# Reads at the head of a two-layer kernel: two queues for the first, Pool for the rest, copies in halves

## The chip, the cores and the metric

The kernel runs on one core of a Trainium2 chip. The metric is device time in microseconds of one execution; the median of several executions counts.

## What is computed

The reference applies two layers, each of them attention and a gated unit with residuals, to 2048 tokens of 448 features in fp32 (16 heads of 28, hidden width 1792). Both layers use the same weights.

```python
def _A_ref(x, wqkv, wo):
    qkv = (x @ wqkv).reshape(B, S, 3, H, Dh).transpose(2, 0, 3, 1, 4)
    q, k, v = qkv[0], qkv[1], qkv[2]
    scores = jnp.einsum("bhqd,bhkd->bhqk", q, k) * (Dh ** -0.5)
    p = _softmax(scores, axis=-1)
    o = jnp.einsum("bhqk,bhkd->bhqd", p, v)
    return o.transpose(0, 2, 1, 3).reshape(B, S, D) @ wo
def _B_ref(x, w_gate, w_up, w_down):
    h = _sigmoid(x @ w_gate) * (x @ w_up)
    return h @ w_down
x = x + _A_ref(_layernorm(x), A_wqkv, A_wo)
x = x + _B_ref(_layernorm(x), B_w_gate, B_w_up, B_w_down)
# the same two lines once more
```

## The kernel before

The 2048 tokens stand as 16 tiles of 128 tokens; four tiles make a block, and there are four blocks. The product of a block with the weights is done in fp16: each operand is split into a high and a low half, and three products are added up. To fit fp16 the weights are scaled by a power of two that is worked out from the sum of their squares. Per layer there are four stages: query, key and value products of all blocks, attention, output product, gated unit. The order of the instructions is written out by hand; each engine (TensorE, VectorE, ScalarE, Pool, and SyncE for transfers) runs its own instructions strictly in that order, and semaphores tie the engines together.

The change is in the head, the work ahead of the first query product:

- `load_x` (line 176) reads tiles of tokens; `load_rows` (lines 211, 213, 214) reads 448 rows of a weight matrix as three slabs of 128 rows and a last one of 64 rows that is read twice. SyncE issues all of them: tokens of tiles 0 to 3 one by one, the query weights (the slabs in two transfers), the key weights, the tokens of block 1, the value weights, the tokens of blocks 2 and 3. Each transfer has one of eight semaphores, in turn, and the ninth waits for the first to have landed.
- `stats` (lines 495, 496) takes mean and variance of a tile on VectorE, and Pool makes the factor of it (498, 500). `scale` (320, VectorE) normalizes the tile, and `turn` (508) transposes it on TensorE, four transposes into four banks of PSUM. Each bank holds one slab of features of all four tiles. The order on VectorE is statistics 0 and 1, scale 0, statistics 2 and 3, scales 1, 2 and 3.
- `turned_high` (530 on VectorE, 532 on ScalarE) copies a bank to fp16, `turned_low` (540, 543) makes the low half.
- `measure_first` (620 on ScalarE, 617 on VectorE) takes the sums of squares of the query weights in three parts, `sum_first` (626) adds them over the partitions on TensorE, and two small operations on VectorE (246, 248) make the power of two.
- `scaled_high` (231, ScalarE) and `scaled_low` (234, VectorE) scale and split the weights by columns. The first query product (564) takes the first 128 columns. `measure` (633) later does for key and value weights in one operation each what `measure_first` does for the query weights.
- `keep_busy` (261) issues products of a zero tile to TensorE between the transposes.
- `tables` (190 to 204) and `ones_of_values` (719, 720) prepare constants on Pool.

## Time and profile before

| | us |
|---|---|
| median of 3 runs | 1894.93 |
| lowest and highest | 1894.68, 1895.23 |
| span of the profiled execution | 1893.0 |
| TensorE busy in it | 1886.5 (100%) |
| VectorE, ScalarE, Pool busy | 1430.7, 1382.7, 231.5 |

The span reaches from the first to the last instruction of one profiled execution; the execution's own time is not given apart from the runs, and its median lies 1.9 us above the span. A row of a timeline gives the start and the duration in us, the engine (PE is TensorE, PEld its loading of weights, DVE VectorE, ACT ScalarE, POOL Pool, SPq SyncE issuing a transfer), the line of the kernel, the operation, what it writes and reads, and in brackets how long the engine had stood idle before it and whose work released it. A row of waits gives the total, the count and the longest.

### The profile page before, as it was taken

Reading aid. Unit: us, or ns where it says so; the run is one execution under the profiler, and the core shown is the slowest. Engines: PE = TensorE matmul, PEld = TensorE weight load, DVE = VectorE, ACT = ScalarE, POOL = GpSimd, SP = SyncE. Lnnn points to the kernel's source line nnn. Section 1 sums busy time; section 2 is a strip of 40 time slices with the busy share of each in tenths; the row PEclk is TensorE's granted clock in tenths of the full one; section 3 lists DMA queues with packets and bytes.
Section 4 is the critical chain, followed back from the end, with each engine's and each line's share of the span. In section 5 each row is a group of like instructions: output and inputs, shape, how many; then the busy total and the mean of one; then the engine's idle time right before and its main releaser. Section 6 shows DMA issues by size and latency. Waiting matters only on the chain. (4 is left out here: it accounts for less than half of the span.)

```text
span 1893.0 us, 56282 instructions
## 1 busy us (share of the span) xinstructions
PE 1886.5 (100%) x24254; PEld 1323.1 (70%) x24254; DVE 1430.7 (76%) x2835; ACT 1382.7 (73%) x1772; POOL 231.5 (12%) x453
## 2 busy tenths in 40 slices
PE   9999999999999999999999999999999999999999
PEld 4455555555556799999954556667666567999998
DVE  7758989898976688787564487787778676887664
ACT  5569999999993566555345799999999745565541
POOL 3023112222101111111100000000000020121110
PEclk9999999999999999999999999999999999999999
DMA  7676454334323566646734322122120245666553
GB/s 247 194 212 166 132 137 128 107 119 129 103 88 121 192 205 235 231 181 238 251 96 134 90 52 47 32 52 52 31 48 24 67 160 174 218 251 223 208 208 142
DMA packets 110882, 270.86 MB, mean 143 GB/s; under 512 B 13214, under 2 KB 67838, under 8 KB 110496
## 3 DMA queue, kind: packets, MB, share of 16 engines
q0 software_dynamic: 31776, 158.51, 23.4%
q1 hardware_dynamic: 78288, 108.20, 20.3%
q8 instruction: 192, 3.15, 0.7%
q10 hardware_dynamic: 560, 0.46, 0.1%
q14 instruction: 66, 0.54, 0.1%
HBM read 207.88 MB, written 50.85 MB: 137 GB/s over the span
## 5 line engine op out<-in xcount | busy, mean ns | idle before, releaser
L1222 ACT ACTIVATE prob_s<-sc 128x1536 f32<-128x1536 f32 (+1 forms) x657 | 887.9, 1487 | 6.6 <-PE sc L1207 5.9
L1258 PE MATMUL acc<-prob_s,val_s 128*32 128x256 f32 (+3 forms) x7700 | 569.9, 383 | 0.0
L1207 PE MATMUL sc<-qp_s 114*32 114x512 f16 x7868 | 553.2, 379 | 0.0
L579 PEld LDWEIGHTS <-gu_s 128*128 128x128 f16 x4368 | 426.9, 98 | 46.8 <-issue 0.4
L1207 PEld LDWEIGHTS <-qp_s 114*32 114x32 f16 x8192 | 272.7, 95 | 203.4 <-issue 88.3
L1258 PEld LDWEIGHTS acc<-prob_s,val_s 128*32 128x32 f32 x7700 | 272.3, 110 | 142.9 <-issue 13.6
L579 PE MATMUL chain<-xwide_s,gu_s 128*128 128x256 f16 x2016 | 247.5, 273 | 0.0
L1552 PE MATMUL dnp<-dn_s,hparts_s 128*128 128x224 f16 x2016 | 225.2, 259 | 0.0
L1552 PEld LDWEIGHTS <-hparts_s 128*128 128x128 f16 x2016 | 194.0, 98 | 4.4
L1238 DVE SCALAR_TENSOR_TENSOR power_q<-power_q,expo_q 128x512 f32<-128x512 f32 x243 | 168.2, 692 | 8.3
L1625 ACT COPY one_q<-chain 128x256 f32<-128x256 f32 x224 | 82.4, 371 | 121.4 <-PE chain L579 120.8
L1641 DVE TENSOR_TENSOR one_q<-side,one_q 128x512 f32<-128x512 f32 x112 | 72.2, 686 | 101.8 <-PE side L579 101.5
L579 PE MATMUL side<-xshort_s,gu_s 128*128 128x256 f16 x1120 | 140.5, 273 | 0.0
L564 PE MATMUL qkp<-xhl_s,wqk_s 128*128 128x512 f16 x616 | 138.1, 379 | 0.7 <-ACT wqk_s L231 0.2
L564 PEld LDWEIGHTS <-wqk_s 128*128 128x128 f16 x616 | 60.1, 98 | 69.8 <-ACT wqk_s L231 1.1
L1437 POOL DMA_DIRECT2D gu_s<-gu_parts x104 | 56.0, 538 | 430.5 <-PE side L579 424.5
L1287 DVE STREAM_TRANSPOSE oturned_q<-acc 128x512 f32<-128x512 f32 x32 | 22.9, 716 | 97.1 <-PE acc L1258 96.9
L1258 PE MATMUL acc<-power_q,val_s 128*32 128x256 f32 (+3 forms) x300 | 94.2, 396 | 0.0
L579 PE MATMUL side<-xwide_s,gu_s 128*128 128x256 f16 x672 | 91.6, 273 | 0.0
L1505 ACT CAST hparts_s<-hsums_q 128x256 f16<-128x256 f32 (+1 forms) x136 | 65.0, 494 | 30.2 <-DVE hsums_q L1517 20.2
L756 ACT ACTIVATE qkhl_q<-qkp 128x512 f16<-128x512 f32 x56 | 33.2, 593 | 71.9 <-PE qkp L564 68.3
L1652 ACT ACTIVATE one_q<-one_q 128x512 f32<-128x512 f32 x56 | 35.2, 629 | 64.3 <-DVE one_q L1641 64.3
(218 smaller groups left out, 2318.0 us busy)
## 6 DMA issues: line engine op xcount, KB each, us to landing
gu_s<-gu_parts POOLq DMA_DIRECT2D x104, 800.0 KB, 6.0
dn_s<-dn_parts POOLq DMA_DIRECT2D x42, 784.0 KB, 7.8
qp_s<-qk_scr SPq DMA_DIRECT2D x96, 224.0 KB
qk_scr<-qkhl_q SPq DMA_DIRECT2D x56, 256.0 KB
gu_parts<-pack_s POOLq DMA_DIRECT2D x14, 800.0 KB, 3.8
xt_scr<-xs_s SPq DMA_DIRECT2D x48, 224.0 KB
xraw_s<-xt_scr SPq DMA_DIRECT2D x12, 768.0 KB
qp_s<-qk_scr SPq DMA_DIRECT2D x64, 112.0 KB
```

The lines of the kernel that those rows point to most:

```text
L564: nc.tensor.matmul(pm, w, x, start=(i == 0), stop=(i == len(terms) - 1))
L579: nc.tensor.matmul(pm, a, x, start=(first and i == 0), stop=(i == len(terms) - 1), skip_group_check=True)
L1207: nc.tensor.matmul(ps[32 * j:32 * j + 32, :], hd.k[:, keys], hd.q[:, qb * W:(qb + 1) * W], start=True, stop=True, tile_position=(0, 32 * j))
L1222: nc.scalar.activation(prob[:, 0:n, :], ps[:, 0:n, :], AF.Exp, scale=exp_scale)
L1238: nc.vector.scalar_tensor_tensor(p, p, c[k], y, op0=ALU.add, op1=ALU.mult)
L1258: nc.tensor.matmul(acc[qb * VC:(qb + 1) * VC, s], v[:, kc % TB, h, :], probs[c * NB + qb][:, s], start=(kc == 0 and a == 0), stop=(kc == N ...
L1437: queue.dma_start(self.gu[-1][m], gu_parts[p, m])
L1505: nc.scalar.copy(to[:, :, 0], a)
L1552: nc.tensor.matmul(pm, a[:, x, t], w[:, p, y], start=(begin and n == 0 and (j == 0 or alone)), stop=(n == 2), skip_group_check=True)
L1625: nc.scalar.copy(to, pm)
L1641: nc.vector.tensor_tensor(one[m], side[m], one[m], op=ALU.add)
L1652: nc.scalar.activation(out, v, AF.Sigmoid, scale=gate_scale)
```

## The change

SyncE issues the tokens of tiles 0 and 2 and the first two slabs of the query weights; ScalarE issues tiles 1 and 3 and the other parts of the query weights, ahead of its table load. All later reads are issued by Pool, in the order key weights, tokens of block 1, value weights, tokens of blocks 2 and 3, behind the factors of the four tiles and ahead of `tables`. The banks are copied to fp16 in two halves of two tiles each: ScalarE copies its three banks for tiles 0 and 1 behind the transposes of tile 1, VectorE copies the first bank for tiles 0 and 1 between scale 2 and scale 3. The first two sums of squares are taken on ScalarE behind these half copies, the second of them behind the half copies for tiles 2 and 3, and the three sums over the partitions stand together. Five products of `keep_busy` go away.

```diff
--- before.py
+++ after.py
@@ -172,12 +172,13 @@
     x_src = x_in[0].rearrange("(p t) d -> p t d", t=NT)
     x_dst = out[0].rearrange("(p t) d -> p t d", t=NT)
 
-    def load_x(t, n):
-        nc.sync.dma_start(x[:, t:t + n, :], x_src[:, t:t + n, :])
-
+    def load_x(t, n, queue=nc.sync):
+        queue.dma_start(x[:, t:t + n, :], x_src[:, t:t + n, :])
+
+    for t in range(TB):
+        load_x(t, 1, (nc.sync, nc.scalar)[t % 2])
     nc.vector.memset(still, 0.0)
     nc.vector.memset(warm, 0.0)
-    nc.scalar.activation(warm, warm, AF.Square)
     make_identity(nc, ident)
     nc.gpsimd.memset(nhalf, -0.5)
     nc.gpsimd.memset(ones, 1.0)
@@ -205,13 +206,13 @@
         big.put(units)
 
 
-    def load_rows(dst, src, c0, n, queue=nc.sync, parted=False):
-
-        for a, b in ((0, 2), (2, 3)) if parted else ((0, 3),):
-            queue.dma_start(dst[:, a:b, :],
-                            src[a * P:b * P, c0:c0 + n].rearrange("(s p) n -> p s n", p=P))
-        queue.dma_start(dst[0:64, 3, :], src[384:448, c0:c0 + n])
-        queue.dma_start(dst[64:128, 3, :], src[384:448, c0:c0 + n])
+    def load_rows(dst, src, c0, n, queue=nc.sync, second=None):
+
+        for a, b in ((0, 2), (2, 3)) if second else ((0, 3),):
+            (second if a else queue).dma_start(
+                dst[:, a:b, :], src[a * P:b * P, c0:c0 + n].rearrange("(s p) n -> p s n", p=P))
+        for r in (0, 64):
+            (second or queue).dma_start(dst[r:r + 64, 3, :], src[384:448, c0:c0 + n])
 
     def split(hi, lo, raw):
 
@@ -520,27 +521,29 @@
                 nc.scalar.copy(self.raw[0:n, kt, :], pt[0:n])
             big.put(self.xn)
 
-        def turned_high(self, kts=range(4), engine=None):
+        def turned_high(self, kts=range(4), engine=None, js=range(TB)):
+            c = slice(js[0] * P, (js[-1] + 1) * P)
             for kt in kts:
                 if kt not in self.pt:
                     continue
-                to, pt = ((self.hi[:, kt, :], self.pt[kt]) if kt < 3 else
-                          (self.tail[0:64], self.pt[kt][0:64]))
+                to, pt = ((self.hi[:, kt, c], self.pt[kt][:, c]) if kt < 3 else
+                          (self.tail[0:64, c], self.pt[kt][0:64, c]))
                 if engine is nc.vector:
                     nc.vector.tensor_copy(to, pt)
                 else:
                     nc.scalar.copy(to, pt)
 
-        def turned_low(self, kts=range(4)):
+        def turned_low(self, kts=range(4), js=range(TB)):
+            c = slice(js[0] * P, (js[-1] + 1) * P)
             for kt in kts:
                 if kt not in self.pt:
                     continue
-                pt = self.pt[kt]
+                pt = self.pt[kt][:, c]
                 if kt < 3:
-                    nc.vector.tensor_tensor(self.lo[:, kt, :], pt, self.hi[:, kt, :],
+                    nc.vector.tensor_tensor(self.lo[:, kt, c], pt, self.hi[:, kt, c],
                                             op=ALU.subtract)
                 else:
-                    nc.vector.tensor_tensor(self.tail[64:128], pt[0:64], self.tail[0:64],
+                    nc.vector.tensor_tensor(self.tail[64:128, c], pt[0:64], self.tail[0:64, c],
                                             op=ALU.subtract)
 
         def drop(self):
@@ -606,7 +609,10 @@
 
         def read(self, j):
             self.raw.append(big.get("wraw", [P, 4, D]))
-            load_rows(self.raw[j], wqkv, j * D, D, parted=(j == 0))
+            if j == 0:
+                load_rows(self.raw[j], wqkv, j * D, D, second=nc.scalar)
+            else:
+                load_rows(self.raw[j], wqkv, j * D, D, nc.gpsimd)
 
         def measure_first(self, i):
 
@@ -1822,15 +1828,9 @@
     wq.tiles()
     first = Block(0)
     begun = [first]
-    for t in range(TB):
-        load_x(t, 1)
     wq.read(0)
-    wq.read(1)
-    load_x(TB, TB)
-    wq.read(2)
-    load_x(2 * TB, 2 * TB)
+    nc.scalar.activation(warm, warm, AF.Square)
     keep_busy(11)
-    wq.measure_first(0)
     first.begin()
     first.turn_banks(4, range(4))
     first.parts()
@@ -1839,24 +1839,32 @@
     for t in range(TB):
         first.scale(t)
         first.turn(t)
-        keep_busy(2)
         if t == 0:
             first.stats(2)
             first.stats(3)
-    wq.sum_first(0)
-    first.turned_high([0], nc.vector)
+            wq.read(1)
+            load_x(TB, TB, nc.gpsimd)
+            wq.read(2)
+            load_x(2 * TB, 2 * TB, nc.gpsimd)
+        if t < TB - 1:
+            keep_busy(2)
+        if t == 1:
+            first.turned_high(range(1, 4), None, (0, 1))
+        if t == 2:
+            first.turned_high([0], nc.vector, (0, 1))
+    wq.measure_first(0)
+    first.turned_high([0], nc.vector, (2, 3))
+    first.turned_high(range(1, 3), None, (2, 3))
     wq.measure_first(1)
     wq.measure_first(2)
-    wq.sum_first(1)
-    first.turned_high([1, 2])
     first.turned_low([0])
+    for i in range(3):
+        wq.sum_first(i)
     keep_busy(2)
-    wq.sum_first(2)
     tables()
-    keep_busy(3)
     wq.high_cols(0, 0, P, slice(0, 1))
     wq.high_cols(0, 0, P, slice(1, 4))
-    first.turned_high([3])
+    first.turned_high([3], None, (2, 3))
     wq.high_cols(0, P, D)
     first.turned_low([1])
     wq.low_cols(0, 0, P)
```

## Prediction

> **What bounds the kernel now.** I read the first part of the page, then who waited for whom on TensorE over the whole run, then the first 25 us engine by engine. The page's first line gives the span:
>
> ```profile
> span 1893.0 us, 56282 instructions
> ```
>
> The median of the runs shown is 1894.93 us, so some 1.9 us lie around this span; I work in the span and add them at the end. These are the waits of TensorE's products but one (the very first product's, for its operand), and they cover all 1893 us:
>
> ```profile
> PE turn L508 <- DVE xn_s L320: 0.8, 1, 0.8
> PE qkp L564 <- ACT wqk_s L231: 0.2, 1, 0.2
> PE qkp L564 <- DVE xhl_s L543: 0.2, 1, 0.2
> ```
>
> All three are in the head. From the first query product on TensorE is never short of work, so a shift of that product should reach the end of the run nearly whole. The product before the change:
>
> ```profile
> 12.99 2.41 PE L564 MATMUL qkp<-xhl_s,wqk_s 128*128 128x512 f16 x9 [0.20 <-ACT wqk_s L231]
> ```
>
> The question is when the changed kernel gets there. No more than the head, 13 us, can be won or lost by it directly.
>
> The chain into 12.99, first VectorE, then ScalarE, then TensorE (start, duration, what it is, and in brackets the idle time and its releaser):
>
> ```profile
> 7.01 0.63 DVE L495 BATCH_NORM_STATS2 st<-x 128x6 f32<-128x448 f32 x1 [0.43 <-DMA x<-in_A_x_dram]
> 7.68 0.18 DVE L496 BATCH_NORM_AGGREGATE mv<-st 128x2 f32<-128x6 f32 x1
> 7.78 0.90 DVE L320 TENSOR_SCALAR xn_s<-x,mv,rs 128x448 f32<-128x448 f32 x2
> 9.12 0.51 DVE L320 TENSOR_SCALAR xn_s<-x,mv,rs 128x448 f32<-128x448 f32 x1 [0.44 <-POOL rs L500]
> 10.42 0.69 DVE L530 CAST xhl_s<-turn 128x512 f16<-128x512 f32 x1 [0.79 <-PE turn L508]
> 11.03 0.61 DVE L617 CUSTOM_DVE_ANT_0 junk_q<-wraw_s 128x448 bf16<-128x448 f32 x1
> 11.56 0.08 DVE L617 DVE_READ_ACCUMULATOR2_ANT first_sums<- 128x1 f32 x1
> ```
>
> ```profile
> 9.07 0.95 ACT L620 ACTIVATE junk_q<-wraw_s 128x896 bf16<-128x896 f32 x1 [6.78 <-DMA wraw_s<-in_A_wqkv_dram]
> 9.93 0.19 ACT L620 ACTIVATION_READ_ACCUMULATOR junk_q<-wraw_s 128x1 f32 x1
> 10.03 0.56 ACT L620 ACTIVATE junk_q<-wraw_s 128x448 bf16<-128x448 f32 x1
> 10.49 0.19 ACT L620 ACTIVATION_READ_ACCUMULATOR junk_q<-wraw_s 128x1 f32 x1
> 10.58 0.56 ACT L532 CAST xhl_s<-turn 128x512 f16<-128x512 f32 x1
> ```
>
> ```profile
> 10.11 0.60 PE L508 MATMUL turn<-ident,xn_s 128*128 128x128 f32 x4
> 10.54 0.59 PE L261 MATMUL still<-still_q 128*128 128x512 f16 x2
> 10.97 0.50 PE L626 MATMUL sums<-first_sums,ones 128*128 128x1 f32 x4
> ```
>
> The reader is to see two strands. Token tile 3 lands at 7.01; behind its statistics stand scale(1), scale(2) and scale(3), the transposes, and the copy at 10.42. The query weights let ScalarE go at 9.07 and are measured by 11.64 (11.56 and 0.08). From there the sum, the power of two and the first scaled columns take 12.99 − 11.64 = 1.35 us.
>
> **The reads.** Four token tiles and the query weights now go out from two queues, and nothing else is read beside them until Pool's factors are done.
>
> ```profile
> 0.80 1.82 SPq L176 DMA_DIRECT2D x<-in_A_x_dram  x4
> ```
>
> Four issues took 1.82 us, 0.455 each, so tile 3 is issued at 1.25 instead of 2.17. But it landed only at 7.01, so the issue was not what it waited for. What the transfers did in that time, and in a later stretch (last two columns: busy share of the DMA engines, GB/s):
>
> ```profile
> 2.00:6.00 4.00, 4.00 (x11) 1.33 (x10) 2.19 (x6) 0.28 (x2) 1.32 (x4) 1.00 0.88 270
> 42.00:46.00 4.00, 4.00 (x21) 1.85 (x19) 2.44 (x8) 1.51 (x3) 1.94 (x3) 1.00 1.05 385
> ```
>
> Tiles 2 and 3 now follow tiles 0 and 1 on two queues, so I expect 2 and 3 to land together. Call that time L. If the engines only share the same work out otherwise, L is 7.0. If two fuller queues fill the idle 12% of 2 to 7 us, L is 6.4. The four tiles are 917 KB: at 270 GB/s from 2.0 they would be through at 5.4, a lower end without any lag. I take L = 6.5, near the filled gaps, and keep 5.4 to 7.0. The Trainium skill, "DMA: Bandwidth & Descriptors", section "Issuing engines are not separate DMA queues", says that reads begun by different engines run on the same 16 DMA engines, interleaved, and that only issue time is saved; by that rule L is 7.0 and the sum below comes out 0.5 us later.
>
> **The chain after L.** VectorE's order is still statistics 2, statistics 3, scale(1). Before, statistics 2 were done while tile 3 was on its way. With both tiles landing at L they stand behind L:
> - Two statistics at 0.77 (7.01 to 7.78): scale(1) starts at L + 1.54, its transposes at + 0.51 = L + 2.05.
> - Transposes plus two warm-keeping products take 0.86 (10.11 to 10.97): transposes of tile 2 at L + 2.91.
> - VectorE's new half copy of the first bank stands ahead of scale(3) in its order and waits for tile 2's transpose of that bank: + 0.31 (10.11 to 10.42) = L + 3.22.
> - The half copy: full ones take 0.61 on VectorE (10.42 to 11.03). The nearest row for 256 columns out of PSUM is ScalarE's, from the page's groups:
>
> ```profile
> L1625 ACT COPY one_q<-chain 128x256 f32<-128x256 f32 x224 | 82.4, 371 | 121.4 <-PE chain L579 120.8
> ```
>
> I take 0.37 (bounds 0.30, half of 0.61, and 0.61): scale(3) at L + 3.59, transposes of tile 3 at + 0.51 = L + 4.10. Tile 2's other three transposes wait for ScalarE's three half copies in the same banks, too. Those run from about L + 2.5 to L + 3.6 and cost the transposes some 0.4 us, less than scale(3) makes tile 3 wait, so nothing more.
> - ScalarE measures the first weight part between its two sets of half copies (0.96, 9.07 to 10.03), done near L + 4.5. Its second set waits for tile 3's transpose of the second bank: 0.31 and one more transpose, 0.15 (a quarter of 0.60), = L + 4.56. Two half copies at 0.37 (bounds 0.28 each, half of 0.56, and 0.56): L + 5.30.
> - The second measurement, which before stood ahead of the copies at 10.03, now follows them: 0.56 and the read of the sum, together 0.65 (10.03 to 10.68): L + 5.95. VectorE's tail measurement ends earlier, near L + 5.4.
> - Sum, power, first columns 1.35, and 0.2 for the second sum product now queued behind this wait (an estimate between nothing and the 0.50 of the pair at 10.97): **first query product at L + 7.5.**
>
> Before, it was at 7.01 + 5.98. The chain behind the tokens is 1.5 us longer: 0.77 for the second statistics, 0.37 for the half copy ahead of scale(3), the rest for the measurement that moved behind the copies. With L = 6.5 the product starts at 14.0, **1.0 us later**; break-even is L = 5.5. The removed five warm-keeping products lie in TensorE's waits and give nothing. ScalarE's five new issues and its table load end near 5 us, inside its idle 6.78.
>
> **The later reads from Pool.** They stand behind the fourth factor: 9.12 before with tile 3 at 7.01, so L + 2.1 after one set of statistics and L + 2.9 after two, 9.4. Pool's price and delay for the same three shapes, and the times at which ScalarE first uses the key and value weights:
>
> ```profile
> 176.44 0.78 POOL L211 DMA_DIRECT2D raw_s<-in_A_wo_dram  x1 [5.59 <-DVE sums L1097]
> 177.21 0.53 POOL L213 DMA_DIRECT2D raw_s<-in_A_wo_dram  x1
> 177.73 0.52 POOL L214 DMA_DIRECT2D raw_s<-in_A_wo_dram  x1
> ```
>
> ```profile
> raw_s<-in_A_wo_dram POOLq DMA_DIRECT2D x1, 672.0 KB, 4.8
> raw_s<-in_A_wo_dram POOLq DMA_DIRECT2D x2, 112.0 KB, 4.4
> ```
>
> ```profile
> 15.08 1.69 ACT L633 ACTIVATE junk_s<-wraw_s 128x1792 bf16<-128x1792 f32 x1
> ```
>
> ```profile
> 23.27 1.68 ACT L633 ACTIVATE junk_s<-wraw_s 128x1792 bf16<-128x1792 f32 x1
> ```
>
> Key weights: last issue at 9.4 + 1.3 = 10.7, landed at 15.1; used at 15.08 + 1.0 = 16.1. The value weights' last issue comes some 2.4 us later, and 2.75 MB at 270 GB/s from 9.9 are through at 20.1; used at 24.3. Eight issues, some 5.2 us, now stand ahead of Pool's tables and memsets, which took from 9.1 to 15.85 and whose first reader is at 23.29:
>
> ```profile
> 15.64 0.21 POOL L720 MEMSET val_s<- 128x64 f32 x1
> ```
>
> ```profile
> 23.29 0.27 PE L735 MATMUL qnorm<-sq_q,ind 128*128 128x256 bf16 x1
> ```
>
> 9.4 + 5.2 + 6.8 = 21.4, still ahead of it. I cost all this at nothing; without that cover it is the second rival.
>
> **Sum.** 1893.0 + 1.0 = 1894.0 us of span, 1895.9 with what lies around it. With L from 6.2 to 7.0 and the bounds of the half copies (−0.25 to +0.6) this case spans 1895.4 to 1896.9. About 0.2%, 3.8 us, is what a measurement of this kernel can tell from no change; the case lies inside.
>
> **Rivals.**
> - *The two queues carry more (not slower).* In 42 to 46 us the engines moved 385 GB/s against 270 in the head, so 270 need not be their limit. At 385 the tiles are through at 4.4; with 0.6 of lag (an estimate between none and tile 3's 1.6, 5.4 to 7.0) L = 5.0, product at 12.5: 1894.4. For it: the share of 0.88. Against: issue was far ahead of landing.
> - *Pool's reads come late (slower).* Under other traffic Pool's reads took much longer:
>
> ```profile
> raw_s<-in_B_w_up_dram POOLq DMA_DIRECT2D x4, 64.0 KB, 9.0
> ```
>
> Key weights at 10.2 + 9.0 = 19.2 would hold ScalarE's measurement 3.1 us beyond 16.1; some 0.9 of it is slack (key columns are scaled at 19.1 behind a sum that TensorE reaches only after tile 1). With the forecast's 1.0 that is 1898.1. It decides from a landing at about 17.0. Against: nothing else is being read then but the rest of the query weights. The Trainium skill, "SBUF — State Buffer", its warning on VectorE blocking DMA, gives a cause: certain VectorE operations lock Pool out of the port through which it writes descriptors. The 0.52 to 0.78 of the three issues above show no such stall.
> - *TensorE starts cold (slower).* The first eleven warm-keeping products:
>
> ```profile
> 1.25 4.87 PE L261 MATMUL still<-still_q 128*128 128x512 f16 x11 [1.25 <-DVE warm L179]
> ```
>
> took 0.44 each, those at 10.54 0.22 in step. With five fewer and longer gaps, a relapse lasting another 4.9 us would cost half of it, 2.4: 1898.3. Against: the longest gap becomes some 1.2 us. The Trainium skill, "TensorE: Matmul & The Clock Gate", Part 1, puts a relapse at an idle window of about 3.4 us; by that rule it does not happen. The granted-clock column stays 1.00 even in the slow products, so products' spacing must be read.
> - *The change does not do what it says:* the order of every engine's instructions shows the moved reads and halves, so no chance of its own.
>
> **Chances.** Forecast 0.58, more from two queues 0.24, late reads from Pool 0.09, cold start 0.05, something not seen 0.04. The range, 1894.1 to 1897.5, holds the first two with their bounds and the milder half of the third. Faster by over 0.2% would need the product before 9.2, ahead of the weights' landing: 0.02. Slower by over 0.2% takes two mishaps together or the unseen: 0.05. Within: 0.93.
>
> **What would show it.** In the changed profile: statistics 2 and 3 back to back from L; a half copy ahead of scale(3); the first query product near 14.0 (12.5 for the first rival); ScalarE's key measurement at once behind its columns (a DMA wait there for the second); products stepping by 0.22 us from the first query tile (0.43 for the third). A product before 12.9 makes the forecast wrong, as does a shift that does not reach the end.

## The result and the profile after

| | before | after |
|---|---|---|
| median of 21 runs, us | 1895.23 | 1898.09 |
| lowest and highest, us | 1894.19, 1896.19 | 1896.17, 1900.30 |
| span of the profiled execution, us | 1893.0 | 1895.7 |
| first query product, us | 12.99 | 14.11 |

The changed kernel takes 1.0015 times as long as before, 95% interval 1.0009 to 1.0021: 2.9 us, where 1.0 was forecast. The kernel before came 0.3 us higher than in the three runs that the forecast started from (1895.23 against 1894.93). Its runs also lie closer together: 2.0 us from lowest to highest, after the change 4.1.

The first line of the page after:

```profile
span 1895.7 us, 56280 instructions
```

The profiled execution is 2.7 us longer, and its own time, 1897.89 us, lies 2.2 us above its span, where the forecast had added 1.9 as before. The rows of its timeline that answer to those of before, first VectorE, then ScalarE (start, duration, work, and in brackets the idle time before it and what ended that):

```profile
4.47 0.63 DVE L496 BATCH_NORM_STATS2 st<-x 128x6 f32<-128x448 f32 x1 [3.27 <-DMA x<-in_A_x_dram]
...
6.74 0.62 DVE L496 BATCH_NORM_STATS2 st<-x 128x6 f32<-128x448 f32 x1
...
8.22 1.06 DVE L321 TENSOR_SCALAR xn_s<-x,mv,rs 128x448 f32<-128x448 f32 x2
...
9.99 0.42 DVE L532 CAST xhl_s<-turn 128x256 f16<-128x256 f32 x1 [0.70 <-PE turn L509]
...
10.33 0.50 DVE L321 TENSOR_SCALAR xn_s<-x,mv,rs 128x448 f32<-128x448 f32 x1
```

```profile
9.23 0.90 ACT L534 CAST xhl_s<-turn 128x256 f16<-128x256 f32 x3 [4.27 <-PE turn L509]
...
11.36 0.65 ACT L534 CAST xhl_s<-turn 128x256 f16<-128x256 f32 x2 [0.29 <-PE turn L509]
...
11.90 0.59 ACT L626 ACTIVATE junk_q<-wraw_s 128x448 bf16<-128x448 f32 x1
```

Statistics 2 start at 6.74 with no transfer in the bracket: they stand behind scale 0, and scale 0 is late because token tile 0 landed at 4.47 instead of 3.48. Tiles 2 and 3 were there by then. From 6.74 the chain runs nearly as forecast, with the second measurement (11.90) behind the copies. Then TensorE:

```profile
12.63 0.60 PE L632 MATMUL sums<-first_sums,ones 128*128 128x1 f32 x4 [0.97 <-ACT junk_q L626]
13.10 0.59 PE L262 MATMUL still<-still_q 128*128 128x512 f16 x2
14.11 6.90 PE L567 MATMUL qkp<-xhl_s,wqk_s 128*128 128x512 f16 x22 [0.42 <-ACT wqk_s L232]
...
20.99 4.26 PE L567 MATMUL qkp<-xhl_s,wqk_s 128*128 128x512 f16 x19
```

The first query product is 1.12 us late. But the first two query tiles, 22 products, take 6.90 us from 14.11, and the next tile starts at 20.99; before, it was 5.55 us from the first product, 12.99, to the same place:

```profile
18.54 4.91 PE L564 MATMUL qkp<-xhl_s,wqk_s 128*128 128x512 f16 x22
```

Why, the seconds of the timeline show, cut into stretches of 1 us (the length of the stretch; the busy time and, in brackets, the number of instructions of TensorE, its weight loading, VectorE, ScalarE and Pool; then the granted TensorE clock as a share of full speed, the busy share of the DMA engines, GB/s):

```profile
13.00:14.00 1.00, 0.69 (x5) 0.20 (x4) 0.69 (x3) 0.35 (x2) 1.00 (x3) 1.00 1.03 412
14.00:15.00 1.00, 0.77 (x3) 0.34 (x4) 0.62 (x2) 1.00 (x4) 0.93 (x4) 0.92 1.16 290
15.00:16.00 1.00, 1.00 (x4) 0.30 (x2) 0.97 (x3) 1.00 (x2) 0.93 (x3) 0.50 0.93 373
16.00:17.00 1.00, 1.00 (x4) 0.34 (x3) 0.96 (x3) 1.00 (x2) 0.93 (x5) 0.50 0.98 400
17.00:18.00 1.00, 1.00 (x4) 0.42 (x3) 1.00 (x1) 0.76 (x2) 1.00 (x1) 0.50 1.02 392
18.00:19.00 1.00, 1.00 (x6) 0.41 (x4) 0.25 (x1) 0.33 (x1) 0.71 (x2) 0.87 0.99 366
```

TensorE ran at half clock from 14.85 to 18.26 (cut to 0.2 us), 3.41 us. So the execution's 2.7 us are 1.1 of the longer chain, 1.3 to 1.4 of the clock (the next tile is 2.45 late), and 0.3 that come at 678 us, of which the last experiment tells.

Every run also gives its mean granted clock to three places. A stretch of 3.41 us at half speed takes 0.0009 of it, so that it reads 0.999. Of the 21 runs after the change 11 read 0.999 or less, median 1898.31; the ten at 1.000 have a median of 1897.15. The kernel before was at 0.999 in 12 of the 114 runs that stood beside the experiments, at 1896.99 to 1898.96, with medians of 1897.7 to 1898.0 where there were two or more in a batch. That is 2.5 us or more above its runs at 1.000 (1895.2 to 1895.3), while 3.41 us at half clock can cost 1.7 at most: such runs seem to be late for another reason as well, which is open. After the change, too, the clock is only one part of the 2.9 us: some 1.9 are left in runs that do not show it.

### The profile page after: what moved, and what is told of

Its sections match the earlier page's. It is cut to its first block, busy times and chain, and to the rows that moved or that the text cites. A ratio compares the mean times of both kernels' runs of the same rounds, so it can differ in the third digit from the quotient of the medians.

```text
span 1895.7 us, 56280 instructions
## 1 busy us (share of the span) xinstructions
PE 1886.7 (100%) x24249; PEld 1325.8 (70%) x24249; DVE 1429.8 (75%) x2836; ACT 1383.4 (73%) x1775; POOL 237.1 (13%) x461
```

## The experiments

Theory: the order of the work delays the first query product by about 1 us, and the five removed `keep_busy` products let the clock fall. The rivals were the reads (two queues, or Pool) and the order alone. Each kernel had eleven runs, e5 and e15 one. No kernel here lies more than 0.2% from before in the median, so most readings rest on profiles, and e1's kernel alone was profiled twice.

| kernel | median | before beside it | ratio, interval | runs at 0.999 or less | first query product |
|---|---|---|---|---|---|
| e1, five products back | 1897.33 | 1895.24 | 1.0010, 1.0001 to 1.0019 | 2 of 11 | 14.18 |
| e2, before without them | 1897.19 | 1895.24 | 1.0011, 1.0002 to 1.0020 | 5 of 11 | 12.77 |
| e3, reads alone | 1895.62 | 1895.24 | 1.0002, 0.9993 to 1.0011 | 3 of 11 | 13.41 |
| e4, order alone | 1896.63 | 1895.24 | 1.0009, 1.0000 to 1.0018 | 5 of 11 | 13.85 |
| e5, as e1 | 1896.53 | 1895.46 | | 0 of 1 | 14.04 |
| e6, pair back | 1897.54 | 1895.46 | 1.0011, 1.0002 to 1.0020 | 4 of 11 | 14.20 |
| e7, three back | 1897.16 | 1895.46 | 1.0009, 1.0000 to 1.0018 | 0 of 11 | 15.01 |
| e8, tokens on a queue of their own | 1898.10 | 1895.46 | 1.0010, 1.0001 to 1.0019 | 8 of 11 | 15.97 |
| e9, before, tail measured first | 1895.71 | 1895.25 | 1.0003, 0.9994 to 1.0012 | 2 of 11 | 13.76 |
| e10, e1 with eight more products | 1897.51 | 1895.25 | 1.0012, 1.0003 to 1.0021 | 0 of 11 | 14.65 |
| e11, e9 with three more products | 1896.07 | 1895.25 | 1.0003, 0.9994 to 1.0012 | 0 of 11 | 14.40 |
| e12, e1 with measurements early | 1896.72 | 1895.25 | 1.0009, 1.0000 to 1.0018 | 3 of 11 | 15.04 |
| e13, before, later reads on Pool | 1895.27 | 1895.31 | 1.0001, 0.9992 to 1.0010 | 2 of 11 | 12.70 |
| e14, e13 with measurements early | 1895.30 | 1895.31 | 0.9998, 0.9989 to 1.0007 | 0 of 11 | 12.75 |
| e15, before, one VectorE instruction more | 1895.27 | 1895.31 | | 0 of 1 | 12.68 |

The last column is of the one profiled execution of each. e15 has the reads and the order of the kernel before, and yet its first query product comes at 12.68 us where before has 12.99:

```profile
12.68 2.41 PE L565 MATMUL qkp<-xhl_s,wqk_s 128*128 128x512 f16 x9 [0.20 <-ACT wqk_s L232]
```

Differences of 0.3 us between two of these profiles are therefore no effect of an edit by themselves.

### e1 and e2: the filling products

e1 puts the five products back into the changed kernel, and the two that had stayed back between the sums; e2 takes the same five out of the kernel before.

```diff
-        if t < TB - 1:
-            keep_busy(2)
+        keep_busy(2)
...
-    for i in range(3):
-        wq.sum_first(i)
-    keep_busy(2)
+    wq.sum_first(0)
+    keep_busy(2)
+    wq.sum_first(1)
+    wq.sum_first(2)
+    keep_busy(3)
```

> The changed kernel with the five warm-keeping products back in their old places (two behind the transposes of tile 3, two between the sums, three ahead of the first query product). Theory (the five removed products let TensorE's clock fall): no stretch of granted clock 0.50, query products in steps of 0.23 us from the first, first product near 14.1 as in the changed kernel, about 1.2 us over the kernel before (1896.4). Rival (the clock falls because the products come late and the gaps are longer, whatever is put between): the 0.50 stays, 1898.1. Rival (the clock is not what costs): 1898.1 with or without the 0.50.

> The kernel before with only these five products removed. Theory: first product at 13.0 as before, then a stretch of granted clock 0.50 and steps of 0.43 us, 1.3 to 1.7 us over the kernel before in most executions, more spread between executions. Rival (late products): no 0.50, the same time as before within 0.3 us.

The first query products of e1:

```profile
14.18 2.41 PE L567 MATMUL qkp<-xhl_s,wqk_s 128*128 128x512 f16 x9 [0.21 <-ACT wqk_s L232]
```

and of e2, with two of its stretches (TensorE's busy time, then granted clock, DMA share, GB/s):

```profile
12.77 6.90 PE L564 MATMUL qkp<-xhl_s,wqk_s 128*128 128x512 f16 x22 [0.45 <-ACT wqk_s L231]
```

```profile
13.00:14.00 1.00, 0.88 (x4) 0.74 0.97 366
14.00:15.00 1.00, 1.00 (x4) 0.50 0.97 366
```

With the products back the fall is gone from the profile, and the first product is as late as without them: the removed products bought no time in the chain. Out of the kernel before, they leave the product where it was (0.22 us earlier, less than e15's difference), and the clock falls at 13.5 us for 3.41 us; the first norm product of the keys is at 32.4 us instead of 31.3. So the clock falls more often without them, from both sides: 5 of 11 runs of e2 against 3 of the 33 of before beside it, 11 of 21 after the change against 2 of 11 in e1. They do not rule a fall out, and e1's median is 0.9 above what was expected of it.

### e3 and e4: the reads and the order by themselves

e3 has the reads of the changed kernel and the order of work before; e4 the order of work after (with the five products gone) and the reads of before.

```diff
# e3: the kernel before, with
+    for t in range(TB):
+        load_x(t, 1, (nc.sync, nc.scalar)[t % 2])
...
+            wq.read(1)
+            load_x(TB, TB, nc.gpsimd)
...
# e4: the changed kernel, with
-        load_x(t, 1, (nc.sync, nc.scalar)[t % 2])
+        load_x(t, 1)
...
-                load_rows(self.raw[j], wqkv, j * D, D, nc.gpsimd)
+                load_rows(self.raw[j], wqkv, j * D, D)
...
```

> Only the reads changed: two queues for tokens and query weights, Pool for the rest; copies, measurements and warm-keeping products in the order of the kernel before. Theory: token 0 lands 1.0 us later (4.5 instead of 3.5) because it shares the engines with token 1, scale(1) at 8.2 instead of 7.8, scale(3) at 9.7 instead of 9.1, first product near 13.6, 0.6 us over the kernel before, clock 1.00. Rival (the faster transfers win more than the shared first tile loses): first product before 12.9, faster than before.

> Only the order changed: half copies, moved measurements, five products fewer; all reads from SyncE as in the kernel before. Theory: tokens as before (scale(1) at 7.8), half copy ahead of scale(3), second measurement behind the copies, first product near 13.6, then the stretch at half clock; 1.9 us over the kernel before. Rival (the late tokens alone make the loss): within 0.3 us of the kernel before.

e3, VectorE's first statistics, and TensorE's first query products:

```profile
4.45 0.63 DVE L496 BATCH_NORM_STATS2 st<-x 128x6 f32<-128x448 f32 x1 [3.25 <-DMA x<-in_A_x_dram]
```

```profile
13.41 2.41 PE L567 MATMUL qkp<-xhl_s,wqk_s 128*128 128x512 f16 x9 [0.20 <-ACT wqk_s L232]
```

Token 0 is again 1.0 late, and the product 0.42, hardly more than executions differ by; the median is 0.4 over before. In e4, with one queue, statistics 2 start at the landing of tile 2, and the product comes 7.46 us later:

```profile
6.39 0.63 DVE L495 BATCH_NORM_STATS2 st<-x 128x6 f32<-128x448 f32 x1 [0.66 <-DMA x<-in_A_x_dram]
```

```profile
13.85 2.41 PE L566 MATMUL qkp<-xhl_s,wqk_s 128*128 128x512 f16 x9 [0.42 <-ACT wqk_s L231]
```

The order alone costs 0.86 us up to the product. This execution kept its clock; five of eleven runs did not.

### e5 to e7: again, and the products in two portions

e5 is e1 profiled once more. e6 puts back only the pair behind tile 3's transposes, e7 only the three behind the last sum (the first part and the second part of e1's diff).

> The kernel with all five filling products back, profiled a second time. Its first profile had the first query product at 14.18 us, products 0.23 us apart, the shift against the kernel before at 1.19 us at the first norm product, 1.76 us at the first bound product of the second block, 2.1 at the end. Theory A (the order of the work makes the 0.9 us that came after the head): the same two steps come again, +0.5 to 0.7 by the bounds (113.2 to 113.6 us) and a span of 1894.9 to 1895.3. Rival (the small waits of TensorE for its own issue between 77 and 105 us differ from execution to execution): the shift at the bounds stays at 1.2 (112.8 us), or differs from 1.76 by over 0.2 either way.

> The change with only the pair of filling products behind tile 3's transposes back. Theory (the clock fell because TensorE had too little to do between 12 and 14 us, where three products are gone and the first one waits): the pair, which runs at about 11.3 to 11.9, lies too early; the clock still falls to 0.50 at 14 to 16 us in about half of the executions, time as the changed kernel, 1897.5 to 1898.2. Rival (any of the five products will do, since activity over the last several us is what counts): clock 1.00 in the products, 1897.3 as with all five back.

> The change with only the three filling products behind the last sum back (two behind the first sum, three behind the last, as before the change). Theory: these cover 12.2 to 13 us, the clock stays at 1.00 in the query products, 1897.3 as with all five back. Rival (the activity counted reaches further back, so all five are wanted): products 0.43 us apart from 14 us on and 1897.5 to 1898.2.

In e5 the shift against before is 1.0 us at the first norm product of the keys (32.3) and 1.0 at the bounds (112.7), where e1 had 1.2 and 1.8. What e1 has more are waits of TensorE's weight loading for its own issue, which e5 does not have:

```profile
99.27 2.15 PEld L567 LDWEIGHTS <-wqk_s 128*128 128x128 f16 x11 [0.28 <-issue]
101.97 2.15 PEld L567 LDWEIGHTS <-wqk_s 128*128 128x128 f16 x11 [0.34 <-issue]
```

So these differ between executions; the rival holds, and 1.4 us of span is what the order and the reads cost with full clock and without such waits, the 0.3 us at 678 us included. Of the two portions the three products at the end seem to matter more: none of e7's eleven runs reads 0.999, four of e6's do. But e7's median is only 0.2 below e1's, and its profile shows one reason. The transposes and filling products of tiles 0 and 1:

```profile
6.96 1.11 PE L509 MATMUL turn<-ident,xn_s 128*128 128x128 f32 x4 [0.83 <-DVE xn_s L321]
7.87 1.06 PE L262 MATMUL still<-still_q 128*128 128x512 f16 x2
8.84 1.11 PE L509 MATMUL turn<-ident,xn_s 128*128 128x128 f32 x4
...
10.57 0.60 PE L509 MATMUL turn<-ident,xn_s 128*128 128x128 f32 x4
```

Four transposes take 1.11 us, from 10.57 on 0.60 (in e1 0.66 at 6.95), and the first query product slips to 15.01. TensorE came up late in this execution, and the clock column reads 1.00 all that time. The trace's own clock records say why: they begin with the first grant of the full clock, which comes at 10.53 us in e7 and at 4.16 to 7.25 us in the other profiles (7.08 before, 4.61 after), and the column counts the time ahead of it as 1.00. Runs at 1.000 are therefore not all free of a slow clock.

### e8: tokens first, on a queue of their own

Tokens alone on SyncE, query weights on ScalarE with its table load written ahead of them (the first issue is at 1.26 us all the same), later reads on Pool, the order of before with the tail rows measured ahead of VectorE's copy. The diff against the changed kernel, without the order:

```diff
-        load_x(t, 1, (nc.sync, nc.scalar)[t % 2])
+        load_x(t, 1)
...
-                load_rows(self.raw[j], wqkv, j * D, D, second=nc.scalar)
+                load_rows(self.raw[j], wqkv, j * D, D, queue=nc.scalar, second=nc.scalar)
...
```

> The order of the work before the change, all filling products kept; the four tokens alone on SyncE's queue, the query weights on ScalarE's queue behind its table load and first activation, later reads on Pool; and the tail rows are measured ahead of VectorE's cast. Theory (the head is set by the tokens' landing and then by the last measurement on the chain to the powers): token 0 lands at 3.5 again, tokens 2 and 3 at 5.7 and 6.5, the last transpose ends by 10.2, the last sum comes at about 11.3 instead of 11.77 and the first query product at 12.2 to 12.7 against 12.99; 1894.4 to 1895.0 where before is 1895.2. Rival (the second queue takes bandwidth from the tokens however late it starts): token 3 lands at 7 or later, the product at 13.0 to 13.5, 1895.2 to 1895.8.

ScalarE's first measurement, VectorE's statistics of tile 3, TensorE's transposes of tile 1, and two stretches of TensorE (columns as for e2):

```profile
5.71 0.95 ACT L626 ACTIVATE junk_q<-wraw_s 128x896 bf16<-128x896 f32 x1 [3.41 <-DMA wraw_s<-in_A_wqkv_dram]
```

```profile
8.39 0.63 DVE L496 BATCH_NORM_STATS2 st<-x 128x6 f32<-128x448 f32 x1 [0.85 <-DMA x<-in_A_x_dram]
```

```profile
9.69 0.80 PE L509 MATMUL turn<-ident,xn_s 128*128 128x128 f32 x4 [2.28 <-DVE xn_s L321]
```

```profile
10.00:11.00 1.00, 1.00 (x6) 0.54 0.00 0
11.00:12.00 1.00, 1.00 (x6) 0.50 0.00 0
```

The rival holds, and more strongly than put: the weights' queue takes its share from the tokens (between 4.0 and 4.5 us ScalarE's queue moved 0.19 MB and SyncE's 0.01), tile 3 lands at 8.39 (7.01 before), TensorE stands idle for 2.28 us, and the clock falls in the transposes. Weights that the kernel before measures at 9.07 are there at 5.71, ahead of tokens that everything waits for.

### e9 to e12: measurements earlier, more filling

e9 is the kernel before with the tail measurement ahead of VectorE's copy; e11 adds three filling products behind tile 0's transposes. e10 is e1 with eight more filling products (the expectation counts seven), e12 is e1 with ScalarE's two measurements ahead of its half copies and VectorE's ahead of its second.

```diff
# e9
-    wq.sum_first(0)
-    first.turned_high([0], nc.vector)
     wq.measure_first(1)
     wq.measure_first(2)
+    wq.sum_first(0)
+    first.turned_high([0], nc.vector)
# e11, and at this place e10
-        keep_busy(2)
+        keep_busy(5 if t == 0 else 2)
# e10
-    keep_busy(11)
+    keep_busy(12)
...
+    keep_busy(3)
     wq.sum_first(0)
...
-    keep_busy(3)
+    keep_busy(4)
# e12
     keep_busy(11)
+    wq.measure_first(0)
+    wq.measure_first(1)
...
-    wq.measure_first(0)
+    wq.measure_first(2)
     first.turned_high([0], nc.vector, (2, 3))
```

> The kernel before the change with one line moved: the measurement of the query weights' tail rows (L617, 0.61 us on VectorE) goes ahead of VectorE's cast of the turned tokens, into the idle 0.79 us that the cast waits for the last transposes. Theory (before the change the chain's last step to the powers was that measurement): last sum at 11.2 to 11.4 instead of 11.77, powers 0.4 to 0.6 earlier, first query product at 12.3 to 12.6 against 12.99; 1894.6 to 1894.9. Rival (ScalarE's casts end at 11.63 and the high parts and the cast of VectorE come no earlier; or TensorE's clock falls more often as its products move together): product at 12.8 to 13.0, 1895.2 to 1895.5.

> The changed kernel with all five filling products back and seven more, put where TensorE still waited: one at the start, three behind tile 0's transposes (while token 2 is waited for), three around the sums, less what lies there. Theory (the clock is taken back where TensorE has too little to do in a stretch of 3.4 us, and granted late where the start has a hole): no execution below full clock after the start, all runs within 1896.4 to 1897.4, median 1896.9. Rival (the 0.9 us that come behind the head in the kernel with five back have nothing to do with the clock): median 1897.3 as there, with the same spread of 1.5 us.

> As the kernel with the tail rows measured first, and three more filling products behind tile 0's transposes, where TensorE waited 0.78 us for token 2 in the profile of before. Theory (nine of 60 runs of the kernel before, at 1897.5 to 1899, are executions in which the clock was taken back): these runs vanish, median as the kernel with the tail rows measured first or up to 0.2 lower, highest under 1896.5. Rival (they come from elsewhere): one or two of eleven above 1897.4 as before.

> The changed kernel with all five filling products back and the three measurements of the query weights moved ahead: ScalarE's two to where the weights land (7.3 us), ahead of all casts, VectorE's ahead of its second half cast. Theory (with all filling back, the rest of the head's delay is that the measurements stand behind the casts, 0.86 us in the profile with the order of the change alone, and token 0, 0.42): last sum with the last transposes, first query product at 12.3 to 12.8, 1.4 to 1.9 us earlier than with the five back alone (14.18), and 1895.0 to 1895.9. Rival (the half casts of ScalarE wait behind the second measurement and push the chain back as much): product at 13.3 to 14, 1896.3 to 1897.2.

e9 failed in a way that neither side had named. Its VectorE rows:

```profile
11.05 0.62 DVE L617 CUSTOM_DVE_ANT_0 junk_q<-wraw_s 128x448 bf16<-128x448 f32 x1 [1.29 <-DMA wraw_s<-in_A_wqkv_dram]
...
12.93 0.15 DVE L246 TENSOR_SCALAR pw<-sums 128x1 int32<-128x1 int32 x1
```

The tail rows land only at 11.05. Before, the copy ahead of the measurement hid that; now the copy, the subtraction and the powers wait behind it, and the product comes at 13.76. e11 has the same, and in its profiled execution tile 3 landed late as well, with one queue:

```profile
8.21 0.63 DVE L495 BATCH_NORM_STATS2 st<-x 128x6 f32<-128x448 f32 x1 [1.75 <-DMA x<-in_A_x_dram]
```

In e10 and e11 no run reads 0.999, which fits the theory that more filling keeps the clock, though 2 of 11 in e1 and in e9 are few to compare with. e11's highest, 1897.51 at full clock, is above the 1896.5 that it forecast. And filling costs what it delays. In e10 the sums now queue behind the filling, the product is at 14.65, and the median is 0.2 above e1's; its runs span 0.9 us (1897.20 to 1898.07) where the changed kernel's span 4.1. For e12 the profiled execution decides nothing on the chain, since its clock fell from 8.7 to 12.2 us:

```profile
8.68 1.10 PE L509 MATMUL turn<-ident,xn_s 128*128 128x128 f32 x4 [0.79 <-DVE xn_s L321]
```

Its median, 0.6 below e1's, has the expected sign and a third of the size; the time of its first product at full clock was not seen.

### e13 to e15: what was left

e13 does one part of the change in the kernel before: later reads on Pool. e14 adds the measurements ahead of the copies, and the powers ahead of VectorE's first subtraction. e15 is the kernel before with one small memset more on VectorE, at the start.

```diff
# e13
-    wq.read(1)
-    load_x(TB, TB)
-    wq.read(2)
-    load_x(2 * TB, 2 * TB)
...
             first.stats(3)
+            wq.read(1)
+            load_x(TB, TB, nc.gpsimd)
+            wq.read(2)
+            load_x(2 * TB, 2 * TB, nc.gpsimd)
...
# e15
-    nc.vector.memset(warm, 0.0)
+    for _ in range(2):
+        nc.vector.memset(warm, 0.0)
```

> The kernel before with one part of the change alone: the later reads (key and value weights, tokens of blocks 1 to 3) begun by Pool behind the token factors; tokens and query weights stay on SyncE's one queue, the order of the work stays. Theory (behind the last query read nothing more is queued, so token 3 and the tail rows land earlier than 7.0 and 11.05 us): first query product 0.2 to 0.6 earlier than 12.99, 1894.6 to 1895.1. Rival (the tokens' landing is set by the query weights queued right behind them, not by the later reads): product at 12.9 to 13.1, 1895.2.

> As the kernel with the later reads on Pool, and all three measurements of the query weights ahead of the casts, the powers ahead of VectorE's first subtraction. Theory (with the later reads out of the way the tail rows land before 10 us, so the measurement fits into the idle time ahead of the cast): last sum at 11.2, powers at 11.4 to 11.7, first query product at 12.0 to 12.4; 1894.0 to 1894.6 against 1895.2. Rival (the tail rows land at 11 us as in the kernel with only the measurement moved, and hold the cast up): product at 13.2 to 13.9, 1895.4 to 1895.9.

> The kernel before with one more instruction on VectorE, a memset of one column at the start, where VectorE is idle. Theory (the 0.3 us near 678 us in every kernel with the halves is VectorE's supply of instructions, which hits another place as its program is one instruction longer): the shift against the kernel before is 0 up to 650 us and +0.2 to +0.4 behind 680 us, with a wait of TensorE's or VectorE's for its own issue there. Rival (the halves themselves, through the buffers they take, make it): no step at 678 us.

e13 and e14, the first query products, and e14's tail measurement:

```profile
12.70 2.40 PE L564 MATMUL qkp<-xhl_s,wqk_s 128*128 128x512 f16 x9 [0.20 <-ACT wqk_s L231]
```

```profile
10.37 0.62 DVE L617 CUSTOM_DVE_ANT_0 junk_q<-wraw_s 128x448 bf16<-128x448 f32 x1 [0.91 <-DMA wraw_s<-in_A_wqkv_dram]
...
12.75 2.46 PE L564 MATMUL qkp<-xhl_s,wqk_s 128*128 128x512 f16 x9
```

The product is 0.3 earlier in these two profiles than in before, but so it is in e15, which leaves the reads alone; single executions with one queue differ by more (tile 3's statistics start at 7.01 in before, 8.21 in e11). What the runs do tell is a cost outside the span. Every run gives its span beside its time, and in e13 the time lies 2.16 us above the span (mean of 11 runs), in the 21 of before beside it 1.91. The same holds throughout: 2.10 to 2.23 us in every run of the kernels whose later reads go out from Pool, 1.84 to 2.02 in every run of those where they stay on SyncE. These reads from Pool cost some 0.2 us that no profile's span contains. e14's expected 12.0 to 12.4 did not come: the tail rows land at 10.37, better than 11.05, but VectorE still waits 0.91 us for them. e14 is no faster than the kernel before. Its eleven runs, though, lie within 1894.85 to 1895.49, where the 21 of before beside it reach 1896.99. No version here is faster than the kernel before by more than the noise.

e3 and e13 differ only in that the first reads go out from two queues or from one, and in ScalarE's table load, which follows its issues in e3. From 2 to 7 us (last two columns: busy share of the DMA engines, GB/s) e3 moved

```profile
2.00:7.00 5.00, 4.28 (x11) 1.00 1.01 348
```

and e13

```profile
2.00:7.00 5.00, 5.00 (x15) 1.00 0.93 293
```

So two queues carry a fifth more here (342 to 348 GB/s in all eight profiles with the tokens on two queues, 281 to 298 in all eight with one), and yet the product comes at 13.41 with two and at 12.70 with one. With two queues the last of these reads is also issued earlier, by 3.43 instead of 4.85 us, and no run separates that from the second queue itself.

e15, VectorE near 678 us, and the same place in the kernel before:

```profile
675.34 0.69 DVE L1642 TENSOR_TENSOR one_q<-side,one_q 128x512 f32<-128x512 f32 x1 [0.92 <-PE side L580]
676.23 0.69 DVE L1642 TENSOR_TENSOR one_q<-side,one_q 128x512 f32<-128x512 f32 x1 [0.20 <-issue]
```

```profile
675.61 1.29 DVE L1641 TENSOR_TENSOR one_q<-side,one_q 128x512 f32<-128x512 f32 x2 [0.92 <-PE side L579]
```

At 674 us e15 ran 0.28 us ahead of the kernel before, from 678 us on 0.02 behind it: a step of 0.30. The same step, 0.3, stands in the profile of every kernel with the half copies, which also have one VectorE instruction more, and in none of those without. One more instruction makes it, in either of the places where one was added.

## Why the prediction was wrong

The forecast was 1895.9 us, the range up to 1897.5, and the median came at 1898.09. By its own steps:

- **That a shift of the first product reaches the end nearly whole** was right: 2.45 us at the third query tile, 2.7 in the span, the difference being the step at 678 us.
- **The chain after L** was right. It put the product 7.5 us behind the second statistics; it is 7.37 in the profile after (6.74 to 14.11) and 7.46 in e4. Scale 3 was put at L + 3.59 and came 3.59 behind 6.74, the half copy at 0.37 and took 0.42, the second measurement was put at L + 5.95, 12.69, and ended at 12.57 (the sum behind it starts at 12.63). That the measurement moved behind the copies lengthens the chain is what e4 shows by itself.
- **The reads** were right in sum (L = 6.5 against 6.74) by luck, since the mechanism was wrong. Tiles 2 and 3 were taken as the late ones; what was late was tile 0, because tile 1 now shares the DMA engines with it from the start: from 1.5 to 3.5 us SyncE's queue moved 0.23 MB and ScalarE's 0.19, while in e13 SyncE's alone moved 0.48. Tile 0's statistics start at 4.40 to 4.57 us in the eight profiles with the tokens on two queues and at 3.36 to 3.55 in the nine with one, e8 among them, whose second queue carries only weights. The prediction had priced four landings as a whole and not the first. (Its sum also lets L begin at 6.2, where the reads had been given as 5.4 to 7.0.) The rival "the two queues carry more" had its premise right (e3 against e13) and its conclusion wrong: more GB/s, a later first tile. The rule of the Trainium skill, "DMA: Bandwidth & Descriptors", section "Issuing engines are not separate DMA queues", that a second issuing engine saves issue time alone, would have to explain 348 against 293 GB/s by reads issued up to 1.4 us earlier; e3 against e13 leaves that open.
- **Pool's later reads at nothing** held inside the span and not outside it. e13 shows the 0.2 us that they cost there; the prediction had taken what lies around the span as unchanged. Inside, the key measurement started without a wait for a transfer, and the last memset ended at 21.3, ahead of its reader at 25.7:

```profile
15.98 1.68 ACT L639 ACTIVATE junk_s<-wraw_s 128x1792 bf16<-128x1792 f32 x1
```

```profile
21.13 0.20 POOL L726 MEMSET val_s<- 128x64 f32 x1
```

- **The step that failed is the clock.** The five removed products were costed at nothing, and the rival that TensorE starts cold got 0.05 and was left outside the range. Its time, 1898.3, is nearly the one that came, but partly by luck: it priced a relapse of 4.9 us at 2.4, and the fall in the profile after lasted 3.41 us and cost 1.3 to 1.4. The ten runs without a recorded fall have their median, 1897.15, inside the range. The rival was set aside on the length of the longest gap. In the 3.41 us ahead of the fall in the profile after that gap is 0.97 us, and the clock fell all the same. TensorE had little work there: it was busy for 1.90 of the 3.41 us ahead of the fall in the profile after, 2.27 in e2, 1.13 in e8 and 1.61 in e12, while the kernel before never has under 2.6 in any such stretch of its profile from 5 us on. But little work alone does not bring a fall. The stretch ahead of it in the profile after, an emptier one of the same profile, and one of e1, both without a fall (columns as for the stretches of 1 us):

```profile
11.44:14.85 3.41, 1.90 (x12) 0.92 (x12) 2.55 (x8) 2.33 (x8) 3.41 (x7) 1.00 0.95 299
5.36:8.77 3.41, 1.19 (x8) 0.60 (x7) 2.98 (x8) 0.00 (x0) 2.56 (x6) 1.00 0.59 208
```

```profile
5.42:8.83 3.41, 1.27 (x8) 0.59 (x7) 2.99 (x8) 0.00 (x0) 2.56 (x6) 1.00 0.61 213
```

What matters besides is where the stretch lies. By the trace's clock records each fall begins a whole number of 3.41 us behind the first grant of the full clock: three times 3.41 in the profile after (4.61 and 14.85 us), twice in e2 (6.66 and 13.49), once in e8 (6.66 and 10.07) and in e12 (5.32 and 8.74). If every profile is cut into pieces of 3.41 us from its first grant on, and the one-column products of the sums are left out of TensorE's busy time, the first three pieces separate in all 17 profiles: 1.13 to 1.61 us in the four ahead of a fall, 1.76 (e1, from 4.93 us) or more in those that no fall follows. With the sums they do not separate (1.91 and 2.27 ahead of the falls of the profile after and of e2). This was read from the traces afterwards and no run was made to test it. The Trainium skill, "TensorE: Matmul & The Clock Gate", Part 1, describes a free-running window of 3413 ns; the four falls recorded here lasted 3.41 us and begin in steps of it, and agree. Its rule that a fall takes an idle window of that length was read as a safe bound, and the traces do not bear that out. That such a window runs on its own also fits that the same program falls in some executions and not in others; no run here set where it lies, so this is argued and not shown.
- **The remark on the clock column** ("stays 1.00 even in the slow products") is right ahead of the first grant (e7) and wrong for a fall later on, which the column shows as 0.50.
- **A term that was missing** is the step at 678 us, 0.3 us, shown by e15.

Put together, in the profiled execution: 1.1 chain and late tile 0, 1.35 clock, 0.3 VectorE's step, 2.7 in the span; the 0.2 us of Pool's reads come on top of it. For the medians less is settled. Of the 1.9 us that runs at 1.000 lie above before, 1.3 are in e5's time too (1896.53 against 1895.23), Pool's 0.2 and VectorE's 0.3 among them. The other 0.6 can come in executions with waits of TensorE for its own issue (e1) or with a late first grant of its clock (e7); how often each occurs is open, since only e1's kernel was profiled twice. Open for the same reason is why the six runs of e2 at 1.000 have a median of 1897.12; its profile has such waits too, and 0.7 us of its loss come where they lie, between 76 and 106 us.

## What to carry to other kernels

Before products that only fill time are taken out, add up how much TensorE has to do in every stretch of some 3.4 us around the place, wherever the stretch begins, and not only how long its longest gap is: here a sparse stretch brought a fall or not by where it lay, so that the same kernel is hit in some executions only. Look at the spread of the runs as well as at the median. A second queue that moves more bytes can still be the slower choice when it lets later data share the engines with the one transfer that everything waits for. Compare times as well as spans: a change can cost outside the span that a profile shows. When a step is moved ahead, ask when its input really lands: the row of before shows only that it was there by the time the engine got to it.

## What the runs showed of the hardware that was not expected

- Four recorded falls of TensorE's clock, each 3.41 us at 0.50 and a whole number of 3.41 us behind the first grant, with gaps of under 1 us in the stretch ahead (profile after) as well as with one of 2.28 us (e8).
- A late start of the clock that the clock column does not show: 1.11 us for four transposes at 6.96 and 8.84 us in e7, 0.60 at 10.57, with the first clock record at 10.53.
- Reads from two queues moved 348 GB/s where the same reads from one moved 293 (e3, e13), and the first tile landed at 4.45 us instead of 3.53.
- Later reads issued by Pool instead of SyncE lengthen the execution by some 0.2 us outside the span: 2.16 us between span and time in e13, 1.91 before.
- One instruction more in VectorE's program makes VectorE wait 0.20 us for its own issue at 676 us, and the kernel 0.3 us longer from there (e15).
